# Layer-norm chunks 2 to 7 enter TensorE with columns on partitions, without transposes

## The chip, the cores and the metric

The kernel runs on one core of a Trainium2 chip. The metric is device time in microseconds (us). The kernel before takes 370.14 us, the median of three runs (369.72 to 371.77). All times of one engine below come from one profiled execution of it, which took 372.47 us in all and whose instructions span 370.3 us.

## The reference

The input `x` has S = 2048 rows and D = 448 columns. Each row is normalised (minus its mean, divided by its standard deviation), and the output is the sum of three parts:

```python
    xn = _layernorm(x, axis=-1)
    return x + _A_ref(xn, A_k, A_v, A_shift_k, A_ssm_k, A_ssm_D) + _B_ref(xn, B_w1, B_b1, B_w2)
```

`_A_ref` is a gated long convolution: a 4-tap causal convolution of `k`, times `v`, then a causal convolution of length 2048 with `ssm_k` for every column (an FFT in the reference), times `xn`. `_B_ref` is a two-layer network, 448 to 1792 to 448, with Mish between the layers. All data is float32.

## The kernel before, in words

The network makes the beat. Rows are cut into 8 **chunks** of 256 (`CH`), the 1792 hidden columns into 7 **pairs** of two 128-column blocks (`NP`). A chunk and a pair make one step of two **slots**, and the program is written out slot by slot (L634 to L648): in the even slot TensorE does the first layer for the pair (`g1_mm`, L457, 22 matmuls of 256 columns); in the odd slot ScalarE does Mish on it and rounds it (`ach`), VectorE computes the rest (`acl`, L75), and TensorE does the second layer for the pair two steps earlier (`g2_mm`, L482 to L484, 12 matmuls of 448 columns). Each product is made of three float32r products (high by high, high by low, low by high), so each operand exists as a rounded high part and a low part. Chunk c is first used in slot 14 c.

The first layer needs the chunk's normalised rows with the 448 columns on partitions: `XH` and `XL`, 128 partitions x 4 blocks x 256 rows. The way there, for chunk c, runs during chunk c - 1: `ln_load` brings the rows (`Q`, tile `qt`, which is also the residual) into SBUF; VectorE takes mean and variance (`bst`, `mv`, L379 to L385); GpSimd raises variance + eps to the power -1/2 (`rstd`, L388) and normalises the rows (`xn`, L392, and a copy of the last 64 columns, L396); then `ln_T` lets TensorE transpose 8 blocks of 128 x 128 into PSUM (L407, four in slot 14 c - 3 ahead of the second layer, four in slot 14 c - 2 ahead of the first layer), ScalarE rounds each half to `XH` (L419), and VectorE computes each half of `XL` (L417). The small VectorE steps of the statistics stand in a list, `drip`, from which `dv()` takes one after each larger VectorE instruction.

Around this beat, the tables at the top of the file place the convolution, which is done as FFT stages by small matmuls: `f1_mm` (L125, first stage, for `ssm_k` in groups `h` and for `k`-taps times `v` in groups `kv`, slots 2 to 60) with `f1_fold` (ScalarE L131, VectorE L132 and L134 on tile `st`) and `f1_out` to DRAM; the taps on VectorE (L162 to L175, one product of four on GpSimd, L155), fed by `k_load` (L145) and `v_load` (L149) on the sync engine's queue; `h2`, `v2`, `prod` and `i1` in slots 63 to 90 (L208 to L262); and `i2` from slot 98 on (`fold` L290 and L292, `i2_mm` L308, `gate` L319). Every engine and every DMA queue takes its instructions strictly in the order in which they are written. The DMA queue of the sync engine (SP) holds the loads of `k`, `v`, `h`, `q`, the intermediate loads and, in slot 14 c + 4, the store of the previous chunk's network result (L494), which waits for VectorE's L489.

Of the kernel before, what the change touches and what calls it, by code (L numbers as in the profile page):

```python
# [7 lines left out]
F32 = mybir.dt.float32  # L8
F32R = mybir.dt.float32r
AF = mybir.ActivationFunctionType  # L10
ALU = mybir.AluOpType
# [6 lines left out]
NP = NF // 2  # L18
# [20 lines left out]
def tile_kernel(ctx: ExitStack, tc, q, k, v, sk, hT, sD, w1, b1, w2, c_f1, c_g, c_gi, c_i2, out):  # L39
    nc = tc.nc  # L40
    V = nc.vector

# [75 lines left out]
    def f1_mm(src, g, key):  # L118
        x = src.pop(g)
        PS[key, g] = ps = [pc(), pc()]  # L120
        for b in range(2):
            for h in range(2):
                for jj in range(2):
                    rg = 32 * (2 * b + h)
                    nc.tensor.matmul(ps[h][64 * jj:64 * jj + 64, b, :D], f1[rg:rg + 32, 0:64], x[rg:rg + 32, jj],  # L125
                                     start=True, stop=True, tile_position=(rg, 64 * jj))

    def f1_fold(g, key):
# [234 lines left out]
    def ln_load(c, eng=None):  # L363
# [3 lines left out]
        else:  # L367
            for jj in range(2):
                nc.sync.dma_start(Q[c][:, jj], q[:, jj])

    def ln_parts(c):
        st = mp.tile([128, 2, 6], F32, name="bst", bufs=2)
        ve = mp.tile([128, 2], F32, name="ve", bufs=2)
        xn = mp.tile([128, 2, D + 64], F32, name="xn", tag="xn", bufs=1)
        XN[c] = xn
        eng = nc.gpsimd if 0 < c < NCHUNK - 1 else V

        def stats(jj):
            V.bn_stats(st[:, jj], Q[c][:, jj])  # L379

        def aggr(jj):
            V.bn_aggr(mv[:, 2 * c + jj], st[:, jj])

        def eps(a, b):
            V.tensor_scalar(ve[:, a:b], mv[:, 2 * c + a:2 * c + b, 1], EPS, None, op0=ALU.add)  # L385

        def power(a, b):
            nc.gpsimd.tensor_tensor(rstd[:, 2 * c + a:2 * c + b], ve[:, a:b], mhalf[:, a:b], op=ALU.pow)  # L388

        def norm(jj):  # L390
            j = 2 * c + jj
            eng.tensor_scalar(xn[:, jj, :D], Q[c][:, jj], mv[:, j, 0:1], rstd[:, j:j + 1],  # L392
                              op0=ALU.subtract, op1=ALU.mult)

        def tail(a, b):
            eng.tensor_copy(xn[:, a:b, D:], xn[:, a:b, D - 64:D])  # L396

        return stats, aggr, eps, power, norm, tail

    def ln_stats(c):  # L400
        stats, aggr, eps, power, norm, tail = ln_parts(c)
        drip.extend([lambda: stats(0), lambda: stats(1), lambda: aggr(0), lambda: aggr(1), lambda: eps(0, 2),
                     lambda: [f(*a) for f, *a in ((power, 0, 2), (norm, 0), (norm, 1), (tail, 0, 2))]])

    def transposes(c, jj, p):
        for kt in range(4):
# [135 lines left out]
    for g in range(-2, 0):  # L542
# [60 lines left out]
    nc.gpsimd.tensor_tensor(ve1, one, mhalf, op=ALU.pow)  # L603
    ln_load(0)
    w1_load(0)
    nc.scalar.dma_start(f1id, c_f1)
    h_load(H_HEAD, nc.scalar)
    w1_load(1)
    nc.sync.dma_start(b1t, b1)
# [43 lines left out]
def _constants():  # L653
# [19 lines left out]
    for kk in range(64):  # L673
# [9 lines left out]
    return dict(c_f1=c(np.stack([f1, np.eye(128)], axis=1)), c_g=c(G.reshape(128, 8, 4, 2, 32)), c_gi=c(GI.reshape(128, 8, 2, 2, 64)),  # L683
                c_i2=c(i2))


# [25 lines left out]
```

## Time and profile before

| | |
|---|---|
| time, median of 3 runs | 370.14 us (369.72 to 371.77) |
| the profiled execution | 372.47 us, of which 370.3 us span and 2.17 us around it |
| TensorE (PE) busy | 362.4 us, 98% of the span |
| VectorE (DVE) busy | 262.9 us, 71% |
| ScalarE (ACT) busy | 166.2 us, 45% |
| GpSimd (POOL) busy | 73.8 us, 20% |
| granted TensorE clock | 0.991 of full speed |
| DMA | 79.35 MB, mean 214 GB/s |

An engine's busy time is the time covered by its instructions. TensorE's matmuls overlap each other by most of their duration, so what one costs is read from the start of one to the start of the next, not from its duration. In the timelines, each row has the start (us from the span's start), the length of the stretch, engine, line, operation, tile written and tiles read, shape and count, and in brackets the engine's idle time before it with what ended it. `SPq` rows are DMAs issued by the sync engine.

### The profile page before, as it was taken

How to read it: one execution, taken by the hardware profiler on the slowest of the kernel's cores; microseconds unless marked ns; L12 is line 12 of the kernel's file. 1: busy time of each engine (PE TensorE's matmuls, PEld its weight loads, DVE VectorE, ACT ScalarE, POOL GpSimd, SP SyncE). 2: the span in 40 equal slices, each digit the busy share in tenths (PEclk: the TensorE clock that was granted, in tenths of full speed). 3: DMA queues.
4: the chain of work that ended last, by engine and by line, in shares of the span. 5: the costliest groups of instructions: out<-in, count | busy, mean ns of one | idle time of the engine just before them, and what ended most of it. 6: DMA issues, size and time to landing. Idle time of an engine off the chain costs nothing.

```text
span 370.3 us, 7468 instructions
## 1 busy us (share of the span) xinstructions
PE 362.4 (98%) x3128; PEld 294.9 (80%) x3128; DVE 262.9 (71%) x358; ACT 166.2 (45%) x277; POOL 73.8 (20%) x59
## 2 busy tenths in 40 slices
PE   6999999999999999999999999999999999999995
PEld 1888889978888989889878666666666889889885
DVE  3799858899999788897605656656285752897751
ACT  2587553334341542352345555556655433235450
POOL 2105100820228221702006000060000005102020
PEclk9699999999999999999999999999999999999999
DMA  8699996838497239433675689897794385959655
GB/s 297 259 269 347 363 363 149 251 115 290 107 295 245 75 76 243 173 83 92 211 239 181 212 228 255 282 267 216 215 306 120 86 249 207 408 204 292 103 71 127
DMA packets 31442, 79.35 MB, mean 214 GB/s; under 512 B 2865, under 2 KB 18098, under 8 KB 31410
## 3 DMA queue, kind: packets, MB, share of 16 engines
q1 hardware_dynamic: 19826, 44.35, 35.4%
q10 hardware_dynamic: 9248, 22.61, 23.4%
q0 software_dynamic: 2336, 11.93, 11.1%
q8 instruction: 24, 0.39, 0.4%
q14 instruction: 8, 0.07, 0.0%
HBM read 50.44 MB, written 28.44 MB: 213 GB/s over the span
## 4 chain that ended last, share of the span: by engine, by line
PE 78%; DVE 9%; DMA 5%; POOL 4%; issue 3%; ACT 1%; DVEq 0%; POOLq 0%; ACTq 0%; SPq 0%
PE pg L457 31%; PE pg L482 10%; PE pg L484 10%; PE pg L483 10%; PE pc L208 7%; PE pc L251 4%; PE pc L125 3%; PE pg L407 2%; DMA x<-in_hT_dram 2%; DVE x L172 2%; PE pc L308 2%; POOL x L155 2%; POOL xn L392 2%; DMA Dkv<-st 1%; DMA av<-Dkv 1%
## 5 line engine op out<-in xcount | busy, mean ns | idle before, releaser
L465 ACT ACTIVATE a<-pg,b1t 128x256 f32<-128x256 f32 x112 | 47.0, 471 | 112.8 <-PE pg L457 97.4
L457 PE MATMUL pg<-XH,w1h 128*128 128x256 f32 x448 | 92.0, 287 | 0.7 <-ACT XH L419 0.7
L457 PEld LDWEIGHTS pg<-XH,w1h 128*128 128x128 f32 x448 | 70.4, 190 | 18.2 <-issue 15.0
L75 DVE TENSOR_TENSOR acl<-a,ach 128x512 fp32r<-128x512 f32 x56 | 38.8, 694 | 63.2 <-ACT ach L74 62.8
L482 PE MATMUL pg<-w2h,ach 128*128 128x448 f32 x224 | 83.0, 370 | 0.0
L484 PE MATMUL pg<-w2h,acl 128*128 128x448 f32 x224 | 81.4, 363 | 0.0
L483 PE MATMUL pg<-w2l,ach 128*128 128x448 f32 x224 | 81.3, 363 | 0.0
L457 PE MATMUL pg<-XL,w1h 128*128 128x256 f32 x448 | 70.2, 279 | 0.0
L457 PEld LDWEIGHTS pg<-XL,w1h 128*128 128x128 f32 x448 | 60.1, 190 | 0.0
L457 PE MATMUL pg<-XH,w1l 128*128 128x256 f32 x336 | 57.3, 279 | 0.0
L482 PEld LDWEIGHTS pg<-w2h,ach 128*128 128x128 f32 x224 | 42.0, 188 | 11.5 <-issue 9.4
L457 PEld LDWEIGHTS pg<-XH,w1l 128*128 128x128 f32 x336 | 47.4, 190 | 0.0
L483 PEld LDWEIGHTS pg<-w2l,ach 128*128 128x128 f32 x224 | 42.1, 188 | 2.6 <-DVE w2l L75 0.2
L484 PEld LDWEIGHTS pg<-w2h,acl 128*128 128x128 f32 x224 | 42.1, 188 | 2.5
L388 POOL TENSOR_TENSOR rstd<-ve,mhalf 128x2 f32<-128x2 f32 (+1 forms) x9 | 9.0, 1003 | 153.5 <-DVE ve L385 148.3
L74 ACT CAST ach<-a 128x512 fp32r<-128x512 f32 x56 | 34.7, 620 | 1.8
L155 POOL TENSOR_TENSOR x<-kr,skb 128x896 f32<-128x896 f32 x8 | 17.0, 2127 | 80.0 <-DVE x L154 59.1
L392 POOL TENSOR_SCALAR xn<-qt,mv,rstd 128x448 f32<-128x448 f32 x12 | 28.5, 2382 | 0.6
L172 DVE TENSOR_TENSOR x<-x 128x896 f32<-128x896 f32 x24 | 26.5, 1105 | 1.0 <-POOL x L155 0.5
L131 ACT COPY st<-pc 128x896 f32<-128x896 f32 x16 | 14.5, 908 | 14.5 <-PE pc L125 14.5
L132 DVE TENSOR_TENSOR st<-pc,st 128x896 f32<-128x896 f32 x16 | 17.4, 1089 | 3.5 <-ACT st L131 3.1
L419 ACT CAST XH<-pg 128x512 fp32r<-128x512 f32 x16 | 9.4, 590 | 21.8 <-PE pg L407 20.4
(71 smaller groups left out, 397.6 us busy)
## 6 DMA issues: line engine op xcount, KB each, us to landing
Dh<-st ACTq DMA_DIRECT2D x16, 448.0 KB, 6.2
Dkv<-st ACTq DMA_DIRECT2D x16, 448.0 KB, 5.2
ah<-Dh SPq DMA_DIRECT2D x8, 896.0 KB, 7.0
av<-Dkv SPq DMA_DIRECT2D x8, 896.0 KB, 5.6
E<-qe ACTq DMA_DIRECT2D x16, 448.0 KB, 5.4
e<-E POOLq DMA_DIRECT2D x8, 896.0 KB, 7.8
kr<-in_k_dram SPq DMA_DIRECT2D x10, 448.0 KB, 6.3
kr<-in_w_dram SPq DMA_DIRECT2D x7, 512.0 KB, 6.5
```

The costliest lines, as they stand in the source:

```text
L74: nc.scalar.copy(h, raw)
L75: V.tensor_sub(l, raw, h)
L132: V.tensor_add(st[:, 0], e, st[:, 1])
L155: nc.gpsimd.tensor_mul(o, KR[g - u // 2], skb[:, u:u + 1].to_broadcast([128, 2, D]))
L172: V.tensor_add(KV[g], KV[g], o)
L208: nc.tensor.matmul(p[32 * t:32 * t + 32, r, :D], g[rs, t, c], a[rs, t], start=True, stop=True, tile_position=(64 * r, 32 * t))
L392: eng.tensor_scalar(xn[:, jj, :D], Q[c][:, jj], mv[:, j, 0:1], rstd[:, j:j + 1], op0=ALU.subtract, op1=ALU.mult)
L457: nc.tensor.matmul(ps[:, n], l, r, start=n_ == 0, stop=n_ == len(mm) - 1)
L465: nc.scalar.activation(a[:, n], ps[:, n], AF.Mish, bias=b1t[:, 2 * p + n:2 * p + n + 1])
L482: nc.tensor.matmul(ps, ah[:, n, cs], w2h[:, f], start=f == 0, stop=False)
L483: nc.tensor.matmul(ps, ah[:, n, cs], w2l[:, f], start=False, stop=False)
L484: nc.tensor.matmul(ps, al[:, n, cs], w2h[:, f], start=False, stop=f == NF - 1)
```

## The change

Chunks 0 and 1 stay as they were. For chunks 2 to 7 the host lays out a second copy of the input, `qT`, with columns on partitions, and the kernel does this, at slots counted from b = 14 (c - 1): the rows are still loaded (b - 2), now only for the statistics and the residual; the turned input is loaded into `xn` (b + 2, 512 KB); the statistics run on VectorE (b + 4), which also negates the two columns of means (`nm`); the negated means and the 1/std are stored to two small DRAM vectors of 256 numbers, `SM` and `SR` (b + 7); a DMA issued by GpSimd reads `SM` for all 128 partitions and 4 blocks and adds it into `xn` (b + 8); a DMA of the sync engine repeats `SR` on all partitions in `idr` (b + 9); VectorE multiplies `xn` by `idr` (after b + 11); ScalarE rounds the product to `XH` and VectorE computes `XL`, each in one instruction of 1024 elements a partition (after b + 12). The transposes, GpSimd's normalisation and the two half splits of these chunks are gone. `idr` shares its SBUF with the identity matrix for the transposes of chunks 0 and 1, so the identity and the matrix `f1` are now loaded by two DMAs at the start.

```diff
+NT = 2
+NT_AT = {"q": -2, "x": 2, "stats": 4, "store": 7, "add": 8, "bcast": 9, "mul": 11, "hi": 12}
...
-    f1id = cp.tile([128, 2, 128], F32, name="f1id")
-    f1, ident = f1id[:, 0], f1id[:, 1]
+    SM = [dp.tile([CH], F32, name="SM") for _ in range(NT, NCHUNK)]
+    SR = [dp.tile([CH], F32, name="SR") for _ in range(NT, NCHUNK)]
+
+    f1 = cp.tile([128, 64], F32, name="f1")
+    idr = cp.tile([128, 1, CH], F32, name="idr")
+    ident = idr[:, 0, 0:128]
...
+    def xT_load(c):
+        XN[c] = xn_tile()
+        nc.sync.dma_start(XN[c], qT[c])
+
+    def nt_stats(c):
+        stats, aggr, eps, power, norm, tail = ln_parts(c)
+        NM[c] = nm = mp.tile([128, 2], F32, name="nm", bufs=1)
+
+        def neg():
+            V.tensor_scalar(nm, mv[:, 2 * c:2 * c + 2, 0], -1.0, None, op0=ALU.mult)
+
+        drip.extend([lambda: stats(0), lambda: stats(1), lambda: aggr(0), lambda: aggr(1),
+                     lambda: (eps(0, 2), power(0, 2)), neg])
+
+    def nt_store(c):
+        dv(len(drip))
+        nc.sync.dma_start(SM[c - NT].rearrange("(j p) -> p j", p=128), NM.pop(c))
+        nc.sync.dma_start(SR[c - NT].rearrange("(j p) -> p j", p=128), rstd[:, 2 * c:2 * c + 2])
+
+    def nt_add(c):
+        nc.gpsimd.dma_start(XN[c], SM[c - NT].partition_broadcast(128).unsqueeze(1).to_broadcast([128, 4, CH]), accum_op=ALU.add)
+
+    def nt_bcast(c):
+        nc.sync.dma_start(idr[:, 0], SR[c - NT].partition_broadcast(128))
+
+    def nt_mul(c):
+        V.tensor_mul(XN[c], XN[c], idr.to_broadcast([128, 4, CH]))
+        dv()
+
+    def nt_split(c):
+        x_tiles(c)
+        nc.scalar.copy(XS[c][0], XN[c])
+        V.tensor_sub(XS[c][1], XN[c], XS[c][0])
+        dv()
...
-                if c + 1 < NCHUNK:
+                if c + 1 < NT:
                     if p == 0:
                         ln_load(c + 1)
...
-                if p == NP - 2 and c + 1 < NCHUNK:
+                if p == NP - 2 and c + 1 < NT:
                     ln_T(c + 1, 0)
...
+    for c in range(NT, NCHUNK):
+        b = 2 * NP * (c - 1)
+        at(b + NT_AT["q"], ln_load, c)
+        at(b + NT_AT["x"], xT_load, c)
+        at(b + NT_AT["stats"], nt_stats, c)
+        at(b + NT_AT["store"], nt_store, c)
+        at(b + NT_AT["add"], nt_add, c)
+        at(b + NT_AT["bcast"], nt_bcast, c)
+        after(b + NT_AT["mul"], nt_mul, c)
+        after(b + NT_AT["hi"], nt_split, c)
...
-    nc.scalar.dma_start(f1id, c_f1)
+    nc.scalar.dma_start(ident, c_id)
+    nc.scalar.dma_start(f1, c_f1)
```

What the change moves in the queues, at three places. In the order rows below, a row has the line, the operation, the tile written and the tiles read, and the shape; lines are those of the kernel that is shown (L75 of before is L80 of the changed one, L145 is L150, L162 to L175 are L167 to L180).

First, VectorE ahead of slot 28, where chunk 2 begins. Before, from the rest of Mish for slot 25 to that for slot 27:

```order
L417 TENSOR_TENSOR XL<-pg_929,XH 128x4x128
L75 TENSOR_TENSOR acl<-a,ach 128x512
L165 TENSOR_TENSOR x<-kr,skb 128x448
L167 TENSOR_TENSOR x<-kr,skb 128x448
L172 TENSOR_TENSOR x<-x 128x896
L175 TENSOR_TENSOR x<-x 128x896
L417 TENSOR_TENSOR XL<-pg_972,XH 128x4x128
L132 TENSOR_TENSOR st<-pc,st 128x896
L134 TENSOR_TENSOR st<-pc,st 128x896
L75 TENSOR_TENSOR acl<-a,ach 128x512
```

In the changed kernel, the same stretch:

```order
L80 TENSOR_TENSOR acl<-a,ach 128x512
L441 TENSOR_TENSOR xn<-xn,idr 128x1024
L170 TENSOR_TENSOR x<-kr,skb 128x448
L172 TENSOR_TENSOR x<-kr,skb 128x448
L177 TENSOR_TENSOR x<-x 128x896
L180 TENSOR_TENSOR x<-x 128x896
L137 TENSOR_TENSOR st<-pc,st 128x896
L139 TENSOR_TENSOR st<-pc,st 128x896
L447 TENSOR_TENSOR XL<-xn,XH 128x1024
L80 TENSOR_TENSOR acl<-a,ach 128x512
```

The multiplication takes the place of the first half of `XL`, and the whole of `XL` now stands behind the two instructions on `st` that the second half stood ahead of.

Second, the sync engine's queue from the store of chunk 0's result (slot 18) on. Before:

```order
L494 DMA out_dram<-qt 128x896
L111 DMA x<-in_hT_dram 128x896
L145 DMA kr<-in_k_dram 128x896
L149 DMA x<-in_v_dram 128x896
L145 DMA kr<-in_k_dram 128x896
L111 DMA x<-in_hT_dram 128x896
```

In the changed kernel:

```order
L539 DMA out_dram<-qt 128x896
L116 DMA x<-in_hT_dram 128x896
L431 DMA SM<-nm 128x2x1
L432 DMA SR<-rstd 128x2x1
L150 DMA kr<-in_k_dram 128x896
L438 DMA idr<-SR 128x256
L154 DMA x<-in_v_dram 128x896
L371 DMA qt<-in_q_dram 128x896
L150 DMA kr<-in_k_dram 128x896
L116 DMA x<-in_hT_dram 128x896
```

The load of `k` for group 1 now stands behind the two small stores, of which the first waits for VectorE's `nm`; the load of `v` for group 1 stands behind `idr`, which waits until `SR` has landed.

Third, VectorE ahead of slot 98, where chunk 7 and the last FFT stage begin (`ex` and `e` are the folds for output chunks 6 and 7). Before:

```order
L417 TENSOR_TENSOR XL<-pg_3535,XH 128x4x128
L290 TENSOR_TENSOR ex<-e_3448 128x896
L292 TENSOR_TENSOR e_3448<-e_3448 128x2x448
L417 TENSOR_TENSOR XL<-pg_3564,XH 128x4x128
L290 TENSOR_TENSOR ex<-e_3450 128x896
L292 TENSOR_TENSOR e_3450<-e_3450 128x2x448
L75 TENSOR_TENSOR acl<-a,ach 128x512
```

In the changed kernel:

```order
L441 TENSOR_TENSOR xn<-xn,idr 128x1024
L295 TENSOR_TENSOR ex<-e_3430 128x896
L297 TENSOR_TENSOR e_3430<-e_3430 128x2x448
L447 TENSOR_TENSOR XL<-xn,XH 128x1024
L295 TENSOR_TENSOR ex<-e_3432 128x896
L297 TENSOR_TENSOR e_3432<-e_3432 128x2x448
L80 TENSOR_TENSOR acl<-a,ach 128x512
```

Two instructions of 512 elements a partition became two of 1024, ahead of the second pair of folds.

More of the change, by code (lines that the diff above doesn't have):

```diff
@@ L38, in tile_kernel @@
 @with_exitstack
-def tile_kernel(ctx: ExitStack, tc, q, k, v, sk, hT, sD, w1, b1, w2, c_f1, c_g, c_gi, c_i2, out):
+def tile_kernel(ctx: ExitStack, tc, q, qT, k, v, sk, hT, sD, w1, b1, w2, c_f1, c_id, c_g, c_gi, c_i2, out):
     nc = tc.nc
@@ L124, in f1_mm @@
                     rg = 32 * (2 * b + h)
-                    nc.tensor.matmul(ps[h][64 * jj:64 * jj + 64, b, :D], f1[rg:rg + 32, 0:64], x[rg:rg + 32, jj],
+                    nc.tensor.matmul(ps[h][64 * jj:64 * jj + 64, b, :D], f1[rg:rg + 32], x[rg:rg + 32, jj],
                                      start=True, stop=True, tile_position=(rg, 64 * jj))
@@ L369, in ln_load, with xn_tile @@
                 nc.sync.dma_start(Q[c][:, jj], q[:, jj])
+    def xn_tile():
+        return mp.tile([128, 4, CH], F32, name="xn", bufs=1)
     def ln_parts(c):
@@ L373, in ln_parts @@
         ve = mp.tile([128, 2], F32, name="ve", bufs=2)
-        xn = mp.tile([128, 2, D + 64], F32, name="xn", tag="xn", bufs=1)
-        XN[c] = xn
+        if c < NT:
+            XN[c] = xn = xn_tile().rearrange("p a b -> p (a b)").rearrange("p (j d) -> p j d", j=2)
         eng = nc.gpsimd if 0 < c < NCHUNK - 1 else V
@@ L403, in ln_stats @@
                      lambda: [f(*a) for f, *a in ((power, 0, 2), (norm, 0), (norm, 1), (tail, 0, 2))]])
+    NM = {}
+    def xT_load(c):
[24 more added lines that the diff above has]
+        dv()
     def transposes(c, jj, p):
@@ L682, in _constants @@
     c = lambda a: np.ascontiguousarray(a, dtype=np.float32)
-    return dict(c_f1=c(np.stack([f1, np.eye(128)], axis=1)), c_g=c(G.reshape(128, 8, 4, 2, 32)), c_gi=c(GI.reshape(128, 8, 2, 2, 64)),
+    return dict(c_f1=c(f1[:, :64]), c_id=c(np.eye(128)), c_g=c(G.reshape(128, 8, 4, 2, 32)), c_gi=c(GI.reshape(128, 8, 2, 2, 64)),
                 c_i2=c(i2))
@@ L693 @@
     lay = lambda x: x.reshape(32, 2, 2, 16, D).transpose(2, 1, 0, 3, 4).reshape(128, NJ, D)
+    rows = np.concatenate([np.arange(D), np.arange(384, D)]).reshape(4, 128)
+    turn = lambda x: x.reshape(128, NCHUNK, 2, D)[..., rows].transpose(1, 4, 3, 2, 0).reshape(NCHUNK, 128, 4, CH)
     kpad = np.pad(a["A_k"][0], ((4, 0), (0, 0)))
     arrs = dict(
-        q=lay(a["A_q"][0]), k=np.concatenate([lay(kpad[:S])[:, :, :][:, :4], lay(a["A_k"][0])], axis=1),
+        q=lay(a["A_q"][0]), qT=turn(lay(a["A_q"][0])), k=np.concatenate([lay(kpad[:S])[:, :, :][:, :4], lay(a["A_k"][0])], axis=1),
         v=lay(a["A_v"][0]), sk=a["A_shift_k"].T, hT=lay(a["A_ssm_k"].T), sD=a["A_ssm_D"][None],
```

## The prediction, made before the changed kernel was run

> **What bounds the kernel now.** I read the page's busy times and its slices first, then the groups by line and shape, then timelines of single engines around the chunk boundaries.
>
> ```profile
> PE 362.4 (98%) x3128; PEld 294.9 (80%) x3128; DVE 262.9 (71%) x358; ACT 166.2 (45%) x277; POOL 73.8 (20%) x59
> ...
> DVE  3799858899999788897605656656285752897751
> ```
>
> TensorE is busy for 98% of the span: time is its instructions end to end, and an edit counts for what it takes from them or makes them wait. VectorE is the engine next to it. Its 40 slices are 9.26 us each; in the ninth to the thirteenth (74 to 120 us, chunks 1 and 2 of the network, where the taps run) it is at 9, with little slack to absorb a wait.
>
> **What is removed.** The timeline of TensorE, with the first group of transposes for chunk 2, the start of chunk 2 in slot 28 (88.23), the first group for chunk 3 and the last for chunk 7:
>
> ```profile
> 78.94 0.60 PE L407 MATMUL pg<-f1id,xn 128*128 128x128 f32 x4
> 79.30 0.45 PE L482 MATMUL pg<-w2h,ach 128*128 128x448 f32 x1
> 79.59 0.37 PE L483 MATMUL pg<-w2l,ach 128*128 128x448 f32 x1
> 79.79 0.36 PE L484 MATMUL pg<-w2h,acl 128*128 128x448 f32 x1
> ...
> 88.23 0.51 PE L457 MATMUL pg<-XH,w1h 128*128 128x256 f32 x3
> ...
> 119.84 0.55 PE L407 MATMUL pg<-f1id,xn 128*128 128x128 f32 x3
> 120.66 0.33 PE L407 MATMUL pg<-f1id,xn 128*128 128x128 f32 x1 [0.28 <-POOL xn L396]
> 120.75 0.45 PE L482 MATMUL pg<-w2h,ach 128*128 128x448 f32 x1
> ...
> 314.17 0.60 PE L407 MATMUL pg<-f1id,xn 128*128 128x128 f32 x4
> 314.52 0.60 PE L457 MATMUL pg<-XH,w1h 128*128 128x256 f32 x3
> ```
>
> From start to start a group of four takes 0.36 us (78.94 to 79.30) or a little less or more; the one at 119.84 takes 0.91, since it waited for GpSimd's `xn`. The twelve groups of chunks 2 to 7, read like this, sum to 5.1 us. The first matmul behind a group also holds up its successor: 79.30 to 79.59 is 0.29, where the usual step is 0.20 (79.59 to 79.79). Nine of the twelve groups stand where this shows: 9 x 0.09 = 0.8. **Removed: 5.9 us.**
>
> Their durations say something else:
>
> ```profile
> L407 PE MATMUL pg<-f1id,xn 128*128 128x128 f32 x64 | 11.0, 299 | 0.3 <-POOL xn L396 0.3
> ```
>
> Charged with its mean duration each, 48 transposes would cost 48 x 0.299 = 14.4 us. They overlap, so I take the starts. The Trainium skill (TensorE: Matmul & The Clock Gate, Part 4: PE-mode transpose) gives about 275 ns for one transpose in a kernel; charged once each, 48 would be an estimated 13.2 us. The trace agrees with that duration, and its starts speak against the charge.
>
> **What is added on VectorE, ScalarE and GpSimd.**
>
> ```profile
> L132 DVE TENSOR_TENSOR st<-pc,st 128x896 f32<-128x896 f32 x16 | 17.4, 1089 | 3.5 <-ACT st L131 3.1
> ```
>
> The rows of `XL` (L417, 512 elements, about 0.69 us, one is shown below) and this one give 0.4 us for 384 elements more, 1.05 ns an element: 1024 elements take 1089 + 134 ns = 1.22 us. Per chunk VectorE loses two halves of `XL` (1.37), and gets a multiplication and one `XL` (2.44) and a small `nm` (0.1): 1.2 us more. ScalarE does one cast of 1024 for two of 512 and is idle for over half its time: I cost it at nothing. GpSimd's normalisation goes, which is off the path but for the 119.84 group; it also slowed VectorE (L172 at 71.83, below).
>
> **Chunk 2, where VectorE has no slack.** Rows of VectorE and of the sync engine's queue, and the landing of a load of `k` from the DMA view of 71 to 72 us:
>
> ```profile
> 68.60 1.08 DVE L172 TENSOR_TENSOR x<-x 128x896 f32<-128x896 f32 x1
> ...
> 71.83 1.50 DVE L172 TENSOR_TENSOR x<-x 128x896 f32<-128x896 f32 x1
> ...
> 74.37 1.18 DVE L162 TENSOR_TENSOR x<-kr,skb 128x896 f32<-128x896 f32 x1
> ...
> 86.18 0.68 DVE L417 TENSOR_TENSOR XL<-pg,XH 128x512 fp32r<-128x512 f32 x1
> ```
> ```profile
> 63.17 1.01 SPq L145 DMA_DIRECT2D kr<-in_k_dram  x1
> ```
> ```profile
> kr<-in_k_dram SPq DMA_DIRECT2D x1, 448.0 KB, 5.1
> ```
>
> `nm` comes just ahead of the L172 of 68.60, so at about 68.7. In the queue both small stores now stand ahead of the load of `k` for group 1, which went out at 63.17 and will go at about 69.8. At 5.1 us, the nearest load in time, it lands at 74.9 (3.5 to 6.3 us are the shortest and the median of such loads on the page: 73.3 to 76.1). The tap at 74.37 reads it. VectorE would be there by 74.0, as L172 drops from 1.50 to 1.08, so it waits until 74.9. From that tap to the second `XL` it took 86.18 - 74.37 = 11.8 us; the first `XL` in between goes (0.6), the multiplication comes (1.2), and the two `st` instructions now stand ahead (2.2): `XL` starts at 74.9 + 11.8 - 0.6 + 1.2 + 2.2 = 89.5 and ends at 90.7. TensorE began chunk 2 at 88.2; without two groups it is there at 87.4, and has seven matmuls (0.8) before it reads `XL`. It **waits 2.5 us** (1.6 to 3.7). Behind that late `XL` stands `acl` of slot 27, not read before slot 31. The load of `v` for group 1, behind `idr`, goes at about 72.5 and is read at 86: covered.
>
> **Chunks 3 to 6.** In chunk 3 VectorE stood idle ahead of its first `XL`:
>
> ```profile
> 121.64 0.69 DVE L417 TENSOR_TENSOR XL<-pg,XH 128x512 fp32r<-128x512 f32 x1 [1.19 <-ACT XH L419]
> ```
>
> That idle takes up the 1.2 us of new work, and from chunk 4 on the slices are lower. I cost these boundaries at nothing; without the cover each costs up to 1.2 us.
>
> **Chunk 7.** The second fold for output chunk 7, and TensorE's first matmul on the folds:
>
> ```profile
> 318.08 1.09 DVE L292 TENSOR_TENSOR e<-e 128x896 f32<-128x896 f32 x1
> ```
> ```profile
> 319.70 0.57 PE L308 MATMUL pc<-ex,i 64*32 64x448 f32 x2
> ```
>
> The fold ended at 319.2 and ends 1.2 later, at 320.4. TensorE reaches L308 at 318.9 without the transposes, and 0.8 later, at 319.7, its second half, which reads this fold: it **waits 0.7 us** (0 to 1.2).
>
> **The start.** `f1id`, now two DMAs, goes out on ScalarE's queue ahead of the load of `h` for which TensorE waits:
>
> ```profile
> 0.94 0.39 ACTq L606 DMA_DIRECT2D f1id<-in_c_f_dram  x1
> ```
> ```profile
> 8.74 0.64 PE L125 MATMUL pc<-x,f1id 32*64 32x448 f32 x8 [2.01 <-DMA x<-in_hT_dram]
> ```
>
> One more issue delays `h` by up to 0.4 us, or not at all if the bytes ahead of it decide: I take 0.2.
>
> **The trip through DRAM.** No row shows a store of single numbers or an accumulating load. The nearest, from the page's DMA issues:
>
> ```profile
> out_dram<-q POOLq DMA_DIRECT2D x5, 448.0 KB, 5.5
> ...
> out_dram<-qt SPq DMA_DIRECT2D x4, 224.0 KB, 1.9
> ...
> qt<-in_q_dram POOLq DMA_DIRECT2D x1, 448.0 KB, 13.1
> ```
>
> The store lies between 1.9 us and some 5 (a load of `k`); I take 2.5. The accumulating load lies between the accumulating store (5.5) and a load queued on GpSimd (13.1); I take 6.5, near the first, as GpSimd's queue is empty then. That is 9 us, of 7.4 to 18. From `nm` (68.7) to the multiplication (82.8 by the sum above) chunk 2 leaves 14. In chunk 4 `nm` stands behind a tap that waited for its `k`, and the multiplication where the first `XL` was:
>
> ```profile
> 148.91 1.09 DVE L162 TENSOR_TENSOR x<-kr,skb 128x896 f32<-128x896 f32 x1 [2.25 <-DMA kr<-in_k_dram]
> ...
> 160.39 0.68 DVE L417 TENSOR_TENSOR XL<-pg,XH 128x512 fp32r<-128x512 f32 x1
> ```
>
> That leaves 160.4 - 150.0 = 10.4 us, and some 2.6 more until TensorE would wait. So the trip is hidden. The Trainium skill (DMA: Bandwidth & Descriptors, Anatomy of one DMA — SWDGE (gpsimd) path) fits a DMA as 2.0 us plus its bytes over 436 GB/s, and warns of a long completion where the target is HBM, as in both small stores. By the fit the trip would be an estimated 5.2 us; no run here shows it yet. The new traffic, 6 x 1.15 MB on 79.35 MB (9%), runs beside loads that land ahead of their use: nothing.
>
> **Sum.** 5.9 - 2.5 - 0.7 - 0.2 = 2.5 us less: the span goes from 370.3 to 367.8, its own execution from 372.47 to 370.0, and the median from 370.14 to **367.6 us**.
>
> **The rivals.**
> - All waits are covered (the `k` load lands early, VectorE without GpSimd beside it catches up): 5.9 less at most 1.5, so 364.2 to 365.7. Against it: the slices at 9. Chance 0.15.
> - The sync queue costs more: loads of `k` and `v` behind `SM`, `SR` and `idr` come late in chunks 3 and 4 as well, for 2 to 4 us: 369.6 to 371.6. For it: the tap at 148.91 waited for its load already; against it: most loads there go out 5 us ahead. Chance 0.18.
> - **Slower:** the trip is long. Each us beyond 13 to 14 stops VectorE at the multiplication, and TensorE behind it, in chunks 2, 3, 4 and 7. At 16 us that is 2 to 3 each, 9 in all: 376.6. The gain is gone from about 14.3 us, and 372.0 is passed at 14.8. For it: the 13.1; against it: the 5.5. Chance 0.15.
> - The transposes cost their durations: 14.4 - 3.4 = 11 less, 359.1. Against it: the starts. Chance 0.02.
>
> **How the numbers follow.** The forecast has 0.50, and 366.3 to 369.2 as its own range. About 0.5% (1.9 us) is what a measurement tells from no change, so 368.3 to 372.0 counts as the same. Faster: 0.38 of the forecast, 0.15 and 0.02, 0.55. Same: 0.12, 0.18 and 0.01 of the long trip, 0.31. Slower: 0.14. The range, 364.0 to 372.0, leaves out the long trip and the whole durations.
>
> **What would show it.** Right: no L407 after 48 us; TensorE waiting at the start of slot 28 for `XL`, and VectorE for `k` ahead of the tap of group 1; L308 waiting for `e`; `xn<-SM` landing after some 6.5 us, and no wait of the multiplication. Wrong: a multiplication that waits for the DMA, or TensorE idle at the starts of chunks 3 to 6.

## The result, and the profile after

The changed kernel takes **435.74 us** (434.14 to 441.17), the kernel before beside it 370.31: a ratio of 1.175, 95% interval 1.169 to 1.180. The forecast of 367.6 and its range up to 372.0 were wrong, on the other side. The profiled execution took 435.02 us, of which 433.2 us span.

The page after, busy times, slices, granted clock and the chain that ended last:

```profile
PE 376.5 (87%) x3080; PEld 298.2 (69%) x3080; DVE 266.3 (61%) x361; ACT 166.2 (38%) x271; POOL 53.7 (12%) x50
...
PE   6999999669998299958993999997689999399996
...
DVE  3799587199983588457821673665076551298661
...
PEclk9899999969999679987997999999979999889999
...
PE 32%; DMA 22%; DVE 7%; ACT 2%; issue 1%; POOL 0%; SPq 0%; ACTq 0%; POOLq 0%
```

TensorE was at 98% and is at 87%, with holes at the starts of chunks 2, 3, 4 and 7 and at loads of the octets in chunks 4 and 5 (the octets are the eight groups of the stages `h2` and `v2`, from slot 63 on, for which the sync engine's queue brings `ah` and `av`). A fifth of the chain is now DMA. In the slices of the larger holes, or just behind them, the granted clock dips to 0.6 to 0.8 as well, and the work there is slower: TensorE is busy for 14 us more than before with 48 matmuls fewer.

What the engines waited for (us in all, times, longest):

```profile
DVE xn L441 <- DMA xn<-SM: 27.5, 4, 7.7
...
DVE x L167 <- DMA kr<-in_k_dram: 16.0, 3, 10.1
...
PE pg L502 <- ACT XH L446: 10.2, 2, 8.2
...
PE pc L213 <- DMA av<-Dkv: 9.0, 2, 6.7
...
PE pc L130 <- DVE st L139: 7.5, 1, 7.5
```

There are two kinds. The multiplication (L441) stands for the add: that is the rival of the long trip. But a tap also stands for `k`, and TensorE for `av`: loads that were there before, and come late now. In this trace both start at the small stores. The sync engine's queue and GpSimd ahead of chunk 2, each row an issue:

```profile
69.50 0.38 SPq L431 DMA_DIRECT2D SM<-nm  x1
69.98 0.50 SPq L432 DMA_DIRECT2D SR<-rstd  x1
70.58 0.64 SPq L150 DMA_DIRECT2D kr<-in_k_dram  x1
82.80 0.33 SPq L438 DMA_DIRECT2D idr<-SR  x1
```
```profile
80.58 1.52 POOL L435 DMA_DIRECT2D xn<-SM  x1 [11.42 <-PE pg L502]
```

GpSimd's add goes out 11.1 us behind the store of `SM`. The bracket names a matmul, but the add reads only `SM` and adds to `xn`, and TensorE makes neither: of what it reads, only `SM` was still on its way. `idr` waits for `SR` until 82.80, 12.8 us. I had taken 2.5. VectorE in the same stretch, and TensorE:

```profile
84.49 1.09 DVE L167 TENSOR_TENSOR x<-kr,skb 128x896 f32<-128x896 f32 x1 [10.06 <-DMA kr<-in_k_dram]
...
92.66 1.23 DVE L441 TENSOR_TENSOR xn<-xn,idr 128x1024 f32<-128x1024 f32 x1 [0.33 <-DMA idr<-SR]
...
99.25 1.21 DVE L447 TENSOR_TENSOR XL<-xn,XH 128x1024 fp32r<-128x1024 f32 x1
```
```profile
90.58 1.79 PE L130 MATMUL pc<-x,f 32*64 32x448 f32 x12 [7.45 <-DVE st L139]
```

The load of `k` behind the two stores landed at 84.5, 13.9 us behind its issue, with the tap waiting for it 10 us; TensorE then waits 7.5 us for VectorE's folds. From the end of `nm` (69.48) to the multiplication the trip took 23.2 us. What the DMA engines did meanwhile is in two windows, one ahead of the stores and one behind (the last two columns: DMA share, GB/s):

```profile
62.00:68.00 6.00, 6.00 (x51) 4.87 (x51) 4.91 (x11) 2.37 (x4) 1.80 (x1) 1.00 0.82 240
74.00:80.00 6.00, 6.00 (x51) 4.88 (x50) 0.43 (x1) 2.19 (x5) 0.00 (x0) 1.00 0.60 22
```

They are 60% busy and move 22 GB/s in the place of 240: whatever is under way nearly stands still. In chunk 3 the multiplication itself is late:

```profile
144.95 1.23 DVE L441 TENSOR_TENSOR xn<-xn,idr 128x1024 f32<-128x1024 f32 x1 [7.68 <-DMA xn<-SM]
```
```profile
147.31 1.01 PE L502 MATMUL pg<-XH,w1h 128*128 128x256 f32 x3 [8.19 <-ACT XH L446]
```

The three matmuls of 1.01 us behind the wait take 0.51 in a row of before (88.23): that is the clock, granted at 0.50 from 147 to 152 us.

### The profile page after: what moved, and what is told of

The parts are those of the page before. It is cut to its first block, busy times and chain, and to the rows that moved or that the text cites. A ratio compares the mean times of both kernels' runs of the same rounds, so it can differ in the third digit from the quotient of the medians.

```text
span 433.2 us, 7406 instructions
## 1 busy us (share of the span) xinstructions
PE 376.5 (87%) x3080; PEld 298.2 (69%) x3080; DVE 266.3 (61%) x361; ACT 166.2 (38%) x271; POOL 53.7 (12%) x50
## 4 chain that ended last, share of the span: by engine, by line
PE 32%; DMA 22%; DVE 7%; ACT 2%; issue 1%; POOL 0%; SPq 0%; ACTq 0%; POOLq 0%
PE pg L502 12%; PE pc L213 5%; DMA E<-qe 4%; PE pg L527 4%; DMA ah<-Dh 4%; PE pg L529 4%; PE pg L528 4%; DMA xn<-SM 3%; DMA SR<-rstd 3%; DMA Dkv<-st 3%; DMA SM<-nm 2%; PE pc L256 1%; PE pc L313 1%; DMA av<-Dkv 1%; DMA kr<-in_k_dram 1%; DMA e<-E 1%
## 5 line engine op out<-in xcount | busy, mean ns | idle before, releaser
L502 PE MATMUL pg<-XH,w1h 128*128 128x256 f32 x448 | 93.9, 292 | 10.9 <-ACT XH L446 10.2
L502 PEld LDWEIGHTS pg<-XH,w1h 128*128 128x128 f32 x448 | 72.2, 195 | 32.7 <-issue 19.3
L527 PE MATMUL pg<-w2h,ach 128*128 128x448 f32 x224 | 84.5, 377 | 0.0
L528 PE MATMUL pg<-w2l,ach 128*128 128x448 f32 x224 | 82.6, 369 | 0.6 <-DVE w2l L80 0.6
L80 DVE TENSOR_TENSOR acl<-a,ach 128x512 fp32r<-128x512 f32 x56 | 38.4, 687 | 64.8 <-ACT ach L79 64.7
L502 PE MATMUL pg<-XL,w1h 128*128 128x256 f32 x448 | 71.9, 283 | 2.5 <-DVE XL L447 2.4
L502 PEld LDWEIGHTS pg<-XL,w1h 128*128 128x128 f32 x448 | 61.4, 194 | 3.3 <-DVE XL L447 3.3
L130 PE MATMUL pc<-x,f 32*64 32x448 f32 x256 | 19.3, 619 | 14.9 <-DVE st L139 7.5
L160 POOL TENSOR_TENSOR x<-kr,skb 128x896 f32<-128x896 f32 x8 | 17.5, 2182 | 89.3 <-DVE x L159 61.3
L396 POOL TENSOR_TENSOR rstd<-ve,mhalf 128x2 f32<-128x2 f32 (+1 forms) x9 | 7.6, 849 | 161.4 <-DVE ve L393 93.0
L441 DVE TENSOR_TENSOR xn<-xn,idr 128x1024 f32<-128x1024 f32 x6 | 7.3, 1225 | 27.8 <-DMA xn<-SM 27.5
L213 PE MATMUL pc<-av,g 64*32 64x448 f32 x256 | 15.4, 593 | 9.0 <-DMA av<-Dkv 9.0
```

The source lines that it names most:

```text
L80: V.tensor_sub(l, raw, h)
L160: nc.gpsimd.tensor_mul(o, KR[g - u // 2], skb[:, u:u + 1].to_broadcast([128, 2, D]))
L213: nc.tensor.matmul(p[32 * t:32 * t + 32, r, :D], g[rs, t, c], a[rs, t], start=True, stop=True, tile_position=(64 * r, 32 * t))
L502: nc.tensor.matmul(ps[:, n], l, r, start=n_ == 0, stop=n_ == len(mm) - 1)
L527: nc.tensor.matmul(ps, ah[:, n, cs], w2h[:, f], start=f == 0, stop=False)
L528: nc.tensor.matmul(ps, ah[:, n, cs], w2l[:, f], start=False, stop=False)
```

## The experiments

Line numbers are those of each run's own kernel. Times are medians, ratios those to the kernel before, run beside it.

### Which part costs what

Theory A was that the 512 single numbers per chunk jam the DMA engines, theory B that the accumulating load is what is late, theory C that the DMAs on the sync queue cost by their number.

**The stores left out.**

```diff
-        nc.sync.dma_start(SM[c - NT].rearrange("(j p) -> p j", p=128), NM.pop(c))
-        nc.sync.dma_start(SR[c - NT].rearrange("(j p) -> p j", p=128), rstd[:, 2 * c:2 * c + 2])
...
-        nc.gpsimd.dma_start(XN[c], SM[c - NT].partition_broadcast(128) ...
+        nc.gpsimd.dma_start(XN[c], sk[0, 0:CH].partition_broadcast(128) ...
```

> Left out: the two small stores of chunks 2 to 7; the accumulating load and the repeated 1/std read two rows of an input instead, so the numbers added and multiplied are not the statistics. All else is the changed kernel. Theory A (the 512 single numbers per chunk, written to DRAM, jam all DMA traffic for about 10 us, and with it the loads behind them): nothing is jammed and the add may go out in its slot, so 367 to 374 us. Theory B (the accumulating load itself, 12 to 16 us in the trace after, is what is late): the multiplications still wait 1 to 4 us each, 380 to 395 us. Theory C (the added DMAs on the sync queue cost by their number): two of the five per chunk are gone, about 405 us.

Measured: 391.7 us, ratio 1.056 (1.051 to 1.062). 44 us of the loss go with the stores, but theory A alone was wrong: what is left lies in B's range, though only one multiplication still waits for the add, 5.2 us.

**The stores alone, in the kernel before.**

```diff
+    def nt_store(c):
+        dv(len(drip))
+        nc.sync.dma_start(SM[c - 2].rearrange("(j p) -> p j", p=128), mv[:, 2 * c:2 * c + 2, 0])
+        nc.sync.dma_start(SR[c - 2].rearrange("(j p) -> p j", p=128), rstd[:, 2 * c:2 * c + 2])
```

> The kernel before, with nothing of the change but the two small stores per chunk (means and 1/std of chunks 2 to 7, four bytes each, into DRAM vectors that nobody reads), in the slots where the changed kernel has them. Theory A: the loads of k, v and the octet loads behind them land some 8 to 10 us late although nobody waits for the stores, so 390 to 420 us. Theory B: two more issues on the sync queue, 370 to 374 us. Theory C: 375 to 385 us.

Measured: 405.3 us, ratio 1.096 (1.092 to 1.099). Twelve DMAs of 1 KB that nobody reads cost 35.6 us: A, and not by a longer trip, since there is none. A window behind the first two of them, and the page's median landing of the loads of `k` (6.3 before):

```profile
69.00:76.00 7.00, 7.00 (x61) 5.87 (x60) 2.14 (x2) 2.37 (x4) 2.27 (x2) 1.00 1.02 40
```
```profile
kr<-in_k_dram SPq DMA_DIRECT2D x10, 448.0 KB, 12.6
```

**The same stores with the numbers 64 bytes apart.** In that kernel, one edit:

```diff
-SM[c - 2].rearrange("(j p) -> p j", p=128)
+SM[c - 2].rearrange("(j p n) -> p j n", p=128, n=16)[:, :, 0]
```

> The kernel before with the same two stores of 256 single numbers per chunk, read by nobody, as in the run that took 405.3 us, but each number 64 bytes behind the one before in a DRAM vector of 16 KB. Theory (what jams is many writes into the same 64 bytes): 369.5 to 373 us. Rival (512 four-byte writes to DRAM jam wherever they go): 400 to 408 us.

Measured: 370.1 us, ratio 1.002 (0.9998 to 1.004), 0.4 us (-0.1 to 1.6), and on its page

```profile
kr<-in_k_dram SPq DMA_DIRECT2D x10, 448.0 KB, 6.0
```

As many numbers from the same engine at the same place cost nothing that can be measured when they don't lie side by side. So neither the count of pieces nor their size alone does it, nor the two issues on the sync queue.

**The stores into SBUF.** As without stores, with `nm` and `rstd` stored to `idr[:, 0, 0:64:32]` and `idr[:, 0, 16:80:32]`.

> As the run without stores, but the two stores are there with the same 512 four-byte pieces per chunk, into a scratch place in SBUF in the place of DRAM (the add and the repeat read input rows, so the statistics are left out). Theory A in its narrow form (single numbers written to DRAM are slow): as without stores, within 4 us, 367 to 378 us. Its rival D (four-byte pieces are slow whatever they go to): as the changed kernel, 420 to 440 us.

Measured: 405.0 us, ratio 1.095 (1.091 to 1.099), between both. The edit has a flaw: the stores go to the tile that the repeat then overwrites, so the repeat waits in the sync queue for them (issue 70.81, repeat 80.63, by the trace), with loads of `k` and `v` behind it. It doesn't tell the theories apart; the price of such a store to SBUF alone is in the first tail below.

**No add either.** As without stores, and the accumulating load gone.

> As the run without stores, and the accumulating loads are left out too (no mean is subtracted; the repeated 1/std still comes by its DMA, from an input row). Theory A2 (what was left at 391.7 us is the accumulating load: 12 to 15 us to landing, and 512 pieces that hold up the loads behind them): 365 to 369 us, so the add's price is 23 to 27 us. Theory C (the repeat of 1/std and the load of the turned input on the sync queue): 380 us and more.

Measured: 371.0 us, ratio 1.003 (1.0004 to 1.005). The add's price is 391.7 - 371.0 = 20.7 us. But 371.0 is not the 365 to 369 that was expected; the start explains it (below).

How the add does it shows at the first octet (slots 61 to 64). Without stores its issue on GpSimd, and the load `av` for that octet, the wait of TensorE for it, and the same load's issue to landing in us, here and without the add:

```profile
190.46 1.31 POOL L433 DMA_DIRECT2D xn<-in_sk_dram  x1
```
```profile
194.76 0.37 SPq L200 DMA_DIRECT2D av<-Dkv  x1
```
```profile
205.66 3.24 PE L213 MATMUL pc<-av,g 64*32 64x448 f32 x32 [6.80 <-DMA av<-Dkv]
```
```profile
av<-Dkv SPq DMA_DIRECT2D x1, 896.0 KB, 10.8
```
```profile
av<-Dkv SPq DMA_DIRECT2D x1, 896.0 KB, 4.7
```

**Plain in the place of added, and large pieces in the place of small.** Both as without stores; the first without `accum_op=ALU.add`, the second with `qT[c]` as the source.

> As the run without stores, with the accumulating load made a plain one: the same 512 pieces of 1 KB from the same input row, issued by GpSimd, written over the turned input in the place of being added (so the input is left out). Theory P (adding in the DMA is what is slow): it lands in 5 to 7 us, 366 to 372 us. Theory Q (512 pieces, all read from one row of 1 KB, are slow however they are written): it lands in 11 us or more, 384 to 393 us.

> As the run without stores, with the accumulating load reading the turned input once more in the place of the repeated row: the same 512 KB are added, in 128 pieces of 4 KB from 128 different places (so twice the input is multiplied, and no mean). Theory P: 11 us or more to landing, 384 to 393 us. Theory Q: 6 to 8 us, 366 to 373 us.

Measured: 383.0 us, ratio 1.036 (1.033 to 1.038), and 379.9 us, 1.027 (1.024 to 1.030). Neither P nor Q: of the add's 20.7 us, 12.0 stay when it is plain and 8.9 when it has large pieces. From issue to landing it still took 10.5 and 9.4 us at the median, 12.7 before the edits.

**Rows of 128 bytes.** The changed kernel, complete; `nm` has 32 columns, the first four hold the two means and the two 1/std, and:

```diff
+        V.transpose(idr[:, 0, 0:32], NM.pop(c))
+        t = idr[:, 0, 0:32].rearrange("(b r) i -> b r i", r=32)
+        for j in range(2):
+            nc.sync.dma_start(SM[c - NT].rearrange("(j b i) -> j b i", j=2, b=4)[j], t[:, j])
+            nc.sync.dma_start(SR[c - NT].rearrange("(j b i) -> j b i", j=2, b=4)[j], t[:, 2 + j])
```

> The changed kernel, complete, with the four columns of numbers turned on VectorE in 32 x 32 blocks first, so that the stores go to DRAM in 16 rows of 128 bytes per chunk in the place of 512 single numbers. Two more DMA issues on the sync queue and about 0.4 us of VectorE per chunk. Theory A: 369 to 380 us, with the add's own 12 us still in the trip. Theory B: 400 to 420 us. Theory that any store and load of the trip costs its latency (some 10 us for a store to DRAM, however it is cut): 425 to 440 us.

Measured: 404.6 us, ratio 1.094 (1.091 to 1.096), worse than theory A had it. The jam is gone (the add goes out 3 to 6 us behind the first store), but the add takes 13.2 us at the median, and four multiplications still wait for it:

```profile
DVE xn L445 <- DMA xn<-SM: 21.4, 4, 8.2
```

At the octets TensorE waits for no load here: `av` went out at 213.94, ahead of the add at 214.91.

**The same, earlier.**

```diff
-NT_AT = {"q": -2, "x": 2, "stats": 4, "store": 7, "add": 8, "bcast": 9, "mul": 11, "hi": 12}
+NT_AT = {"q": -7, "x": -1, "stats": -1, "store": 1, "add": 3, "bcast": 4, "mul": 11, "hi": 12}
```

> The complete version with the 128-byte rows (404.6 us), with the rows loaded 5 slots, the turned input 3, the statistics 5, the stores 6, the add and the repeat 5 slots earlier, so that the trip has some 14 us more before its multiplication. Theory L (only the length of the trip counted there): no multiplication waits, 366 to 372 us. Theory D (the add also holds up other loads wherever it runs): 380 to 392 us.

Measured: 392.5 us, ratio 1.061 (1.057 to 1.066). No multiplication waits any more, and 22 us are lost all the same, so the length of the trip was not all: D rather than L. The 22 us are not the add's alone: the start has its part (below), and the stores, the repeat and the turned columns are still there. At an octet TensorE waits 6.5 us for `ah`, a load that has no part in the change.

### Prices with nothing beside them

Two kernels that do what the kernel before does and then run a tail of DMAs, each waiting for the one ahead to land, so that the step from issue to issue is its price.

> The kernel before with a tail behind its end, in which nothing else runs: small stores and repeated loads of several shapes one after the other, each waiting for the one ahead to land, so that issue to issue is the price of one; the time grows by the tail and isn't compared. Single numbers, 256 of 4 bytes to one DRAM vector: theory A 4 to 6 us, against 2 us for 128 pieces of 64 bytes and for a row of 1 KB. If it is writing into the same 64 bytes again and again, the 256 numbers 64 bytes or 1 KB apart cost 2 to 3 us; if every small write to DRAM costs, they cost the same 4 to 6. To SBUF: about 2 us. Repeated and accumulating loads of 512 KB: sync queue plain 4 us, GpSimd plain 5, accumulating 6 to 8, repeated 7 to 10, both 9 to 12 us. A load of 448 KB issued about 1 us behind 256 single numbers: 4 us without them, 8 us or more with them.

> The kernel before with another tail behind its end, one DMA after the other; the time isn't compared. 256 single numbers next to each other 8 to 9 us, 128 of them half of that, at 8, 16, 32 bytes from each other 4, 2.5, 2 us, 64 bytes apart 1.8. Plain loads of 512 KB on the sync queue: 128 pieces of 4 KB 3.2 us; 512 pieces of 1 KB from 512 places 4 us if the number of pieces is nothing and 8 us if it is what made the repeated row slow (8.4); 128 pieces of 4 KB from one 4 KB row: 8 us if reading one place again is what is slow. A load of 448 KB beside 256 numbers 64 bytes apart: 3.5 to 4.5 us; beside the repeated accumulating load: 7 us or more.

Small stores in the first tail, on the sync queue: 256 adjacent numbers (L670), 64 bytes apart (L671), 1 KB apart (L672), 128 pieces of 8 bytes side by side (L673), 128 of 64 bytes (L674):

```profile
375.03 0.37 SPq L670 DMA_DIRECT2D W<-src  x1
384.18 0.36 SPq L671 DMA_DIRECT2D W<-src  x1
385.95 0.36 SPq L672 DMA_DIRECT2D W<-src  x1
387.50 0.33 SPq L673 DMA_DIRECT2D W<-src  x1
390.58 0.33 SPq L674 DMA_DIRECT2D W<-src  x1
392.00 0.32 SPq L675 DMA_DIRECT2D W<-src  x1
```

9.2 us for 1 KB of adjacent numbers (7.6 for the same store ahead of it, issued at 367.42); 1.8, 1.6, 3.1 and 1.4 for the others. 256 numbers to SBUF, two to a partition and 128 bytes apart, took 2.0 (395.50 to 397.47). A load of 448 KB from elsewhere, on ScalarE's queue, alone and beside 256 adjacent numbers (VectorE's copy waits for it):

```profile
447.32 0.69 DVE L690 COPY U<-U 128x1024 f32<-128x1024 f32 x1 [3.51 <-DMA U<-in_q_dram]
...
459.86 0.69 DVE L694 COPY U<-U 128x1024 f32<-128x1024 f32 x1 [11.12 <-DMA U<-in_q_dram]
```

So a queue that has nothing to do with the stores is nearly stopped with them. The second tail has the same load beside 256 numbers 64 bytes apart, and beside the repeated accumulating load on GpSimd's queue (from its issue to its landing; alone it took 3.6 there):

```profile
455.73 0.69 DVE L694 COPY U<-U 128x1024 f32<-128x1024 f32 x1 [3.63 <-DMA U<-in_q_dram]
```
```profile
U<-in_q_dram ACTq DMA_DIRECT2D x1, 448.0 KB, 6.2
```

So the numbers apart cost a neighbour nothing, and the add slows it, to 6.2 us where 7 or more was expected. Also in the second tail come the spacings (L669 side by side, 256; L670 128 of them; L671 8 bytes apart, L672 16), and loads of 512 KB: 512 pieces of 1 KB from 512 places (L679), the same from one row (L680), 128 pieces of 4 KB from one row (L681):

```profile
368.30 0.38 SPq L669 DMA_DIRECT2D W<-src  x1
376.38 0.32 SPq L670 DMA_DIRECT2D W<-src  x1
385.68 0.37 SPq L671 DMA_DIRECT2D W<-src  x1
390.35 0.37 SPq L672 DMA_DIRECT2D W<-src  x1
391.92 0.36 SPq L673 DMA_DIRECT2D W<-src  x1
...
403.80 0.37 SPq L679 DMA_DIRECT2D U<-W  x1
407.53 0.37 SPq L680 DMA_DIRECT2D U<-W  x1
416.18 0.33 SPq L681 DMA_DIRECT2D U<-W  x1
420.14 0.33 SPq L682 DMA_DIRECT2D U<-W  x1
```

8.1 us side by side, 4.7 at 8 bytes, 1.6 at 16. Half as many numbers side by side took 9.3, not half: the time isn't a price per number, and its rule stays open. Nor does the time lie in the packets: by that run's DMA view all 272 packets recorded behind the issue at 368.30 lie between 369.0 and 369.6 us, and then there is none up to 376.3. What the landing waits for in these 6.7 us no trace shows. For the loads: 3.7 us from 512 places, 8.7 from one row of 1 KB, 4.0 from one row of 4 KB. What makes the repeat slow is reading the same 1 KB 512 times, not the number of pieces alone.

### The start

**The constants by two DMAs**, alone in the kernel before:

```diff
-    nc.scalar.dma_start(f1id, c_f1)
+    nc.scalar.dma_start(f1id[:, 1], c_f1[:, 1])
+    nc.scalar.dma_start(f1id[:, 0], c_f1[:, 0])
```

> The kernel before with one thing of the change: the constants come by two DMAs in the place of one, ahead of the load of h on ScalarE's queue. By the prediction 0 to 0.4 us; by the starts of the profiles (TensorE's first network matmul at 13 to 14.6 us in the changed kernels, 12.3 and 9.5 with one DMA) 1 to 2.5 us, 371 to 372.5 us.

Measured: 373.8 us, ratio 1.009 (1.006 to 1.012), 3.3 us (2.1 to 4.4): more than either number. `h` goes out at 1.84 in the place of 1.37, now behind the first load of weights (1.63 in before). TensorE's first matmuls on `h` in its trace, and in that of the run with the numbers 64 bytes apart, whose start is that of the kernel before:

```profile
8.94 1.80 PE L125 MATMUL pc<-x,f1id 32*64 32x448 f32 x16 [3.02 <-DMA x<-in_hT_dram]
```
```profile
6.93 1.01 PE L127 MATMUL pc<-x,f1id 32*64 32x448 f32 x16
```

The delay is not that of the issue alone: `h` takes 7.0 us to land here. In the profiled execution of before it took 7.2, although it went out at 1.37; that is the row at 8.74 which the prediction reads. In four traces with the same order at the start (stores alone, numbers apart, both tails) it took 4.2 to 4.4, and these matmuls begin at 6.0 to 6.9 us without a wait. The clock adds to it: from 8 to 16 us it was granted at 0.50 here, 0.60 in the profiled before and 1.00 in the four. Why `h` lands late in one execution and early in another isn't shown.

**`h` ahead of the constants**, in the kernel before, and in the run without stores and add:

> The kernel before with two lines at the start exchanged: on ScalarE's queue the load of h goes out ahead of the load of the constants. If the order of the issues against the weight loads on the sync queue sets when h lands (the split of the constants, which put h one issue later, cost 3.3 us), h lands earlier: 367 to 369.3 us. Otherwise 369.4 to 370 us.

> As the run without stores and without the add (371.0 us; no mean is subtracted and the repeated 1/std is an input row), with the load of h ahead of the two constant loads on ScalarE's queue. If the split start is what keeps that run above the kernel before (its price alone was 3.3 us), 367 to 368.7 us, which is the forecast of 367.6 without the trip. Otherwise 370.5 to 371.5 us.

Measured: 369.6 us, ratio 0.9995 (0.998 to 1.001), so going out earlier than before gains nothing there; and **366.6 us, ratio 0.991 (0.988 to 0.994)**, 4.5 us below the run with the split start. With the trip and the start taken out, the rest of the change gains 3.4 us; this kernel leaves out the means and the true 1/std, so it shows what the rest is worth and is no version to use. Its row at chunk 2:

```profile
86.40 0.73 PE L500 MATMUL pg<-XL,w1h 128*128 128x256 f32 x4 [0.91 <-DVE XL L445]
```

### A complete version that would keep the gain

Four tries to feed the multiplication without single numbers and without an accumulating load: the columns turned on VectorE, 16 rows of 128 bytes stored, one repeat of a row of 2 KB (means and 1/std) into the place of the coming `XL`, the mean subtracted by GpSimd, `h` first at the start:

```diff
+        V.transpose(T, nm)
+        for r in range(4):
+            nc.sync.dma_start(SMR[c - NT].rearrange("(r b i) -> r b i", r=4, b=4)[r], t[:, r])
+    def nt_bcast(c):
+        nc.sync.dma_start(XS[c][1][:, 0:2].bitcast(F32), SMR[c - NT].partition_broadcast(128) ...
+    def nt_sub(c):
+        nc.gpsimd.tensor_sub(XN[c], XN[c], XS[c][1][:, 0:1].bitcast(F32).to_broadcast([128, 4, CH]))
```

> A complete version made from what the runs so far show: four columns of numbers turned on VectorE and stored as 16 rows of 128 bytes, one load on the sync queue that repeats means and 1/std on all partitions (128 pieces of 2 KB, into the place that the low half of the chunk will take), the mean subtracted by GpSimd in SBUF, no accumulating DMA; rows, turned input and statistics at the early slots; at the start the load of h ahead of the two constant loads. Theory (single-number stores, accumulating load and start are all that the change lost): 365.5 to 369 us. Rival (the added DMAs and the added VectorE work cost as much as the transposes): 370 to 374 us.

> The complete other way (379.6 us) put back to the slots of the changed kernel for rows, turned input and statistics; repeat one slot behind the stores, subtraction on GpSimd two slots behind that. Its second layer waited at two places for VectorE, where the early statistics had come on top of other work. Theory (with the repeat at some 5 us in the place of 12 and the stores at 2 to 3 in the place of 10 the trip fits into the slots that the change gave it): 365.5 to 369.5 us. Rival (the added work on VectorE and the issues on the sync queue cost more than the transposes at any place): 372 to 380 us.

> The complete other way at nearly the usual slots (384.4 us), with the four stores of 128-byte rows and the repeat issued by GpSimd in the place of the sync engine, and rows, turned input, statistics and stores two slots earlier. Theory (what that version lost is that the repeat waits in the sync queue for the stores to land, with the loads of k and v behind it: VectorE's tap stood 8.4 us for k): 365.5 to 369.5 us. Rival (VectorE's added work itself is too much at the boundaries): 373 to 382 us.

> The complete other way with the trip on GpSimd's queue (391.0 us), with one number changed: the repeat is issued one slot later, so that GpSimd's product of a tap stands ahead of it and no longer waits behind it for the stores to land. Theory (each of these versions loses its time to whatever stands in order behind the DMA that waits): the two stalls of 8 to 9 us at chunks 2 and 3 go, 370 to 376 us. Rival (the stalls come from the added work): 385 us and more.

Measured: 379.6 us at the early slots, ratio 1.025 (1.021 to 1.030); 384.4 at the usual ones, 1.040 (1.038 to 1.043); 391.0 with stores and repeat on GpSimd's queue, 1.058 (1.054 to 1.061); 378.2 with the repeat one slot later, 1.023 (1.021 to 1.024), a little above what was expected. The first three lie above their theory and their rival; none beats the kernel before. In the second the repeat (L438) waits in the sync queue for the four stores, and `k` goes out behind it; VectorE's tap then stands:

```profile
67.07 4.47 SPq L434 DMA_DIRECT2D SMR<-T  x4
72.76 0.33 SPq L438 DMA_DIRECT2D XL<-SMR  x1
73.19 0.38 SPq L150 DMA_DIRECT2D kr<-in_k_dram  x1
```
```profile
79.29 2.25 DVE L167 TENSOR_TENSOR x<-kr,skb 128x896 f32<-128x896 f32 x1 [8.35 <-DMA kr<-in_k_dram]
```

On GpSimd's queue the tap's product (L160) stood behind the waiting repeat instead. One slot number, which only puts the repeat behind that product, gave back 12.8 us, and TensorE's two stalls of 7.4 and 7.7 us for the taps are gone from its trace. Its longest waits there are 3.8 us for `XL`, 2.5 for `ah` at an octet and 1.3 for the identity matrix at the start; the last 8 us over the kernel before were not taken apart by a run.

## Why the prediction was wrong, step by step

**The trip through DRAM, "9 us, of 7.4 to 18", is the step that failed.** It took 23.2 us in chunk 2 (nm's end to the multiplication) and 25.7 in chunk 3 (119.29 to 144.95). Both terms were off. The store of single numbers, 2.5 us by the store of a 224 KB tile, takes 7.6 to 9.2 with nothing beside it and 11 in the kernel: the row had nothing of what sets the price, numbers side by side. The accumulating load, 6.5 us by an accumulating store and GpSimd's plain ones, takes 11.7 to 16.2 in the kernel; 13.1 was among the rows, and I chose the other end because GpSimd's queue was empty, where the queue was not the reason: with nothing beside it the add still takes 8.9.

**"The new traffic runs beside loads that land ahead of their use: nothing" failed too, and is the larger part.** I priced bytes. The stores are 1 KB each and cost 35.6 us with no reader; the add costs 20.7 with no store ahead of it. The Trainium skill (DMA: Bandwidth & Descriptors, Back-pressure in remote DMA) says, for transfers between cores, that writes which stall also stall the other queues of the engine that sends them. The runs show the like within one core: the load on another queue took 3.5 us alone and 11.1 beside a store of 256 adjacent numbers. That stalled writes are the reason isn't shown.

The same page (Specifications) says that below 512 bytes a DMA engine reads, modifies and writes. By that all small stores of the tail should be slow; 128 pieces of 64 bytes took 1.4 us and numbers 16 bytes apart 1.6. So smallness alone isn't the price here, and the measurement decides. Nor does its fit for GpSimd's path (Anatomy of one DMA — SWDGE (gpsimd) path) hold for this add: an estimated 3.2 us for 512 KB, where the repeated add took 8.9 alone (430.89 to the next issue at 439.79, by the first tail's trace) and a plain load of 128 pieces 3.5.

**The transposes: right.** By the starts of the pairs' first matmuls in the run without stores and add, the groups gave back 0.9, 1.2, 1.0, 0.8, 0.8 and 0.8 us, 5.5 in all, against 5.9.

**The added work: right.** The multiplication takes 1.23 us and the whole `XL` 1.21, against 1.22 each.

**Chunk 2: the right place and the wrong size.** `k` did go out behind the two stores (70.58; I had 69.8) and the tap did wait for it, but `k` took 13.9 us and not 5.1. In the changed kernel TensorE waits 7.45 us for the folds there and 0.86 for `XL`; with the stores and the add gone, 0.91 for `XL`, against 2.5.

**Chunks 3 to 6 at nothing: wrong** with the trip (8.2 us in chunk 3, and 4.8 and 2.0 around the start of chunk 4), right without it. **Chunk 7, 0.7: right.** Without the trip (366.6 us), TensorE's load of weights for the second half of L313 waits for the second fold:

```profile
315.37 0.11 PEld L313 LDWEIGHTS pc<-e,i 64*32 64x32 f32 x2 [0.70 <-DVE e L297]
```

The first matmul behind L313 is 0.66 us later there, counted from the first one of the pair ahead, than in before. **The start, 0.2: wrong**, 3.3; the bound of 0.4 was the length of one issue, and what grew was the time until `h` landed, and with it the wait and the low clock behind it.

**The rivals.** The long trip had the right mechanism but a chance of 0.15, a price for a trip of 16 us only (376.6), and none for what the trip does to other loads. Its places were nearly right: the multiplication waits for the add in chunks 3, 4, 6 and 7, and in chunk 2 behind a tap that had waited for `k`. The sync queue's cost came as well. Sum by the runs: -3.4 for the rest of the change, +4.5 for the start, +20.7 for the add, +35.6 for the stores gives 427.4 us from 370.0; the 8.3 us up to 435.7 come when both stand in one trip, and were not shown apart.

## What to carry to other kernels

Price a DMA by its pieces and its addresses, not by its bytes: before adding one, find a row with the same piece size and the same neighbourhood, and where there is none, measure it in a tail of its own. Ask of a slow transfer not only who waits for it but what else is on the DMA engines and what stands in order behind it in each queue; the loss here lay with loads that have no part in the change. If a column of numbers must cross partitions by way of DRAM, don't store it number beside number: turning it first (32 x 32 on VectorE) and storing rows took the changed kernel from 435.7 to 404.6 us, though no version here came below the kernel before.

## What the hardware did that I had not expected

- 256 numbers of 4 bytes side by side take 7.6 to 9.2 us to store to DRAM, though the packets recorded of them are over within 1.3 us of the issue, and nearly stop other queues meanwhile (22 GB/s); 16 bytes or more apart they take 1.6 to 2.7, and 64 bytes apart they cost the kernel nothing that can be measured.
- Reading one row of 1 KB 512 times takes 8.7 us, 512 different ones 3.7. That a load adds costs less: with large pieces it takes 5.3 us from issue to landing in the place of 3.5 on GpSimd's queue, by the first tail's trace.
- One more issue of 0.4 us ahead of `h` at the start cost 3.3 us: `h` took 7.0 us to land, where it took 4.2 to 4.4 in four traces with the order of before, and the clock was low behind the wait.
- Behind a stall of TensorE the granted clock was low (0.50 in the 5 us from 147 us on in the changed kernel, which begin as the wait of 8.2 us ends), so this stall cost more than its length.
